# Four heads at a time: chunk bounds from a chunk-per-partition load, bounds in column tiles, and the FFN interleaved in a fixed order

## The chip, the cores and the metric

The kernel runs on one core of a Trainium2 chip. The metric is device time in microseconds (us), where lower is better. The profile is one execution; its span, from the first to the last instruction, is one to two us shorter than the time that is reported. Engines are named as in the profile: PE is the matmul engine (TensorE), PEld its weight loads, which overlap PE (busy 57% and 85% of the span of before), DVE is VectorE, ACT is ScalarE, POOL is GpSimd and SP is SyncE. "Clock" is the TensorE clock that the throttle granted, as a share of full speed; these traces show it at 1.00 or 0.50, and other values are means over a stretch.

A program on one core has no second die to compare with, so a run counts as slow only if it is over 1.5% above the fastest run of the same kernel.

## The reference

The first half is attention with chunk selection, for 4 batches of 8 heads, 768 positions and head size 64. The second half is a gated FFN on the 3072 x 512 result. Cut to what matters:

```python
k_chunks = k.reshape(B, H, 24, 32, 64)                   # 24 chunks of 32 keys
k_min, k_max = k_chunks.min(axis=3), k_chunks.max(axis=3)
ub = sum_d max(q_d * k_min_d, q_d * k_max_d)             # upper bound per query and chunk
ub = where(causal, ub, -1e9)
top_chunks = argsort(ub)[..., -6:]                       # six chunks per query
scores = (q @ k.T) / 8, masked to the selected chunks and to i >= j
x = softmax(scores) @ v                                  # then heads side by side: 3072 x 512
out = (sigmoid(x @ w_gate) * (x @ w_val)) @ w_out        # d_ff = 1536
```

Because max(q k_min, q k_max) is relu(q) k_max + relu(-q) (-k_min), the bound is one matmul with a contraction of 128 rows: relu(q) stacked on relu(-q), against k_max stacked on -k_min. It is done in fp32 in both kernels, since the selection depends on it; everything after it is fp16.

## The kernel before

Work goes head by head, in a software pipeline of three steps. `phase1a` transposes q and k of a head (fp32, on PE), forms the relu stack on ACT and reduces k to chunk bounds on DVE, from the transposed copy in PSUM:

```python
        qkT = pqk.tile([128, S], F32, tag="qkT", name=f"qkT_{hs}")
        for sb in range(NB):                                                   # NB = 6 blocks of 128
            nc.tensor.transpose(qkT[:, 128 * sb:128 * sb + 128], qk_nat[:, sb, :], ident32)
        # ... Qcat = relu(q), relu(-q) on ACT; headK, headQ: fp16 copies on DVE ...
        kTv = qkT[64:128, :].rearrange("p (a c) -> p a c", a=NC)
        nc.vector.tensor_reduce(Kcat[0:64, :], kTv, AX.X, ALU.max)
        nc.vector.tensor_reduce(Kcat[64:128, :], kTv, AX.X, ALU.min, negate=True)
```

`phase1b` makes the bounds and picks six chunks. The queries are the weights here, so six loads of 128 x 128 fp32 weights serve matmuls of only 24 columns each (in the trace each load and each matmul shows as two: 12 of each per head). The picked set goes back through PE into 24 extra rows of the fp16 score operands, so that unselected chunks get a large negative score:

```python
        for qb in range(NB):
            nc.tensor.matmul(ubp[:, qb, :], Qcat[:, 128 * qb:128 * qb + 128], Kcat,
                             start=True, stop=True)
        # ... add the causal penalty, MAX8 per block, compare with the sixth value -> Ap ...
        for qb in range(NB):
            nc.tensor.transpose(ApT[:, 128 * qb:128 * qb + 128], Ap[:, qb, :], ident16)
        nc.vector.tensor_copy(headQ[64:88, :], ApT)
```

`phase2` computes transposed scores per key block, adds the causal mask of the diagonal block with an extra matmul, and multiplies with v:

```python
                nc.tensor.matmul(sc, headK[:, 128 * jb:128 * jb + 128], headQ[:, i0:i1],
                                 start=True, stop=not has_diag)
                if has_diag:
                    off = 128 * jb - i0
                    nc.tensor.matmul(sc[:, off:off + 128], ident16, tneg, start=False, stop=True)
                a_t = attnp.tile([128, n], F16, tag="attnT", name=f"at_{hs}_{jb}_{i0}")
                nc.scalar.activation(a_t, sc, AF.Exp)
        # ... 21 matmuls of 65 columns: attention times value; normalise; transpose pairs of heads ...
```

The FFN of a batch becomes available when its eighth head is done. The main loop issues five FFN units as a block after each head until the queue is empty; 30 units last for six of the eight heads:

```python
    for i in range(NHEADS + 2):
        # ... phase1b(i - 1), phase2(i - 2), loads, phase1a(i) ...
        nunits = min(len(pending_ffn), 5) if i < NHEADS else len(pending_ffn)
        for _ in range(nunits):
            pending_ffn.pop(0)()
```

The softmax here doesn't subtract the row's maximum and nothing guards it: scores larger than these inputs give would overflow.

Of the kernel before, what the change touches and what calls it, by code (L numbers as in the profile page):

```python
# [8 lines left out]
F32 = mybir.dt.float32  # L10
F16 = mybir.dt.float16
BF16 = mybir.dt.bfloat16
# [4 lines left out]
NEG = -30000.0  # L17
# [3 lines left out]
def kernel(  # L21
# [15 lines left out]
    NB = S // 128  # L37
    D_FF = moe_w_gate.shape[1]
    NFB = D_FF // 128
    scale = 1.0 / (D ** 0.5)  # L40
    NHEADS = B * H

    consts = ctx.enter_context(tc.tile_pool(name="consts", bufs=1))
    stage = ctx.enter_context(tc.tile_pool(name="stage", bufs=3))
    persist = ctx.enter_context(tc.tile_pool(name="persist", bufs=1))
    att = ctx.enter_context(tc.tile_pool(name="att", bufs=3))
    smalls = ctx.enter_context(tc.tile_pool(name="smalls", bufs=6))
    attnp = ctx.enter_context(tc.tile_pool(name="attnT", bufs=20))
    xpool = ctx.enter_context(tc.tile_pool(name="xpool", bufs=8))
    xnatp = ctx.enter_context(tc.tile_pool(name="xnat", bufs=2))  # L50
    hglup = ctx.enter_context(tc.tile_pool(name="hglu", bufs=26))
    pqk = ctx.enter_context(tc.tile_pool(name="pqk", bufs=1, space=bass.MemoryType.PSUM))
    pa = ctx.enter_context(tc.tile_pool(name="pa", bufs=5, space=bass.MemoryType.PSUM))
    pb = ctx.enter_context(tc.tile_pool(name="pb", bufs=1, space=bass.MemoryType.PSUM))
# [5 lines left out]

    tneg = consts.tile([128, 128], F16, tag="tneg")
    nc.gpsimd.memset(tneg, 0.0)
    nc.gpsimd.affine_select(
        out=tneg, in_=tneg, compare_op=ALU.is_ge, fill=NEG,
        base=0, pattern=[[1, 128]], channel_multiplier=-1,
    )
    Epat = consts.tile([24, NC, CH], F16, tag="Epat")
    nc.gpsimd.memset(Epat, 0.0)
    nc.gpsimd.affine_select(
        out=Epat, in_=Epat, compare_op=ALU.not_equal, fill=NEG,  # L70
        base=0, pattern=[[-1, NC], [0, CH]], channel_multiplier=1,
    )
    Edram = nc.dram_tensor("E_scratch", (24, S), F16, kind="Internal").ap()
    nc.sync.dma_start(Edram, Epat.rearrange("a b c -> a (b c)"))
    pen = consts.tile([24, NC, CH], F32, tag="pen")
# [3 lines left out]
        base=0, pattern=[[1, NC], [0, CH]], channel_multiplier=-1,  # L79
    )  # L80
    pen2 = consts.tile([128, NB, 24], F32, tag="pen2")
    penv = pen.rearrange("a b c -> a (b c)")
    for qb in range(NB):
        p2ps = pa.tile([128, 24], F32, tag="m", name=f"pen2t_{qb}")
        nc.tensor.transpose(p2ps, penv[:, 128 * qb:128 * qb + 128], ident32[0:24, 0:24])  # L85
        nc.vector.tensor_copy(pen2[:, qb, :], p2ps)  # L86

    wg16 = persist.tile([128, 4, D_FF], F16, tag="wg16")
    wv16 = persist.tile([128, 4, D_FF], F16, tag="wv16")
    wo16 = persist.tile([128, NFB, 512], F16, tag="wo16")  # L90
    _wunits = []
    for sl, dst, nchunk in ((moe_w_gate, wg16, 4), (moe_w_val, wv16, 4), (moe_w_out, wo16, NFB)):
        src = sl.rearrange("(c p) f -> p c f", p=128)
        for c in range(nchunk):
            def _load(src=src, dst=dst, c=c):
                st = stage.tile([128, src.shape[2]], F32, tag="wstage")
                nc.sync.dma_start(st, src[:, c, :])
                nc.scalar.copy(dst[:, c, :], st)  # L98
            _wunits.append(_load)

    def score_chunks(jb):
        lo = 128 * jb
        if jb == 0:
            return [(0, 384), (384, 768)]
        if jb == 1:
            return [(128, 384), (384, 768)]
        return [(lo, 768)]

    st1 = {}
    xT = {}  # L110
    xnat = {}
    hgl_tiles = {}

    def phase1a_dma(hs):
        b, hh = divmod(hs, H)
        d = {}
        qk_nat = stage.tile([128, NB, 128], F32, tag="qk_nat", name=f"qknat_{hs}")
        nc.sync.dma_start(qk_nat[:, :, 0:64], q[b, hh].rearrange("(sb p) d -> p sb d", p=128))
        nc.sync.dma_start(qk_nat[:, :, 64:128], k[b, hh].rearrange("(sb p) d -> p sb d", p=128))
        v_nat = stage.tile([128, NB, 64], F32, tag="v_nat", name=f"vnat_{hs}")  # L120
        nc.sync.dma_start(v_nat, v[b, hh].rearrange("(sb p) d -> p sb d", p=128))
        d["qk_nat"] = qk_nat
        d["v_nat"] = v_nat
        return d

    def phase1a(hs, d):
        b, hh = divmod(hs, H)
        qk_nat = d["qk_nat"]
        v_nat = d["v_nat"]
        v16 = att.tile([128, NB, 65], F16, tag="v16", name=f"v16_{hs}")  # L130
        nc.gpsimd.tensor_copy(v16[:, :, 0:64], v_nat)
        nc.gpsimd.memset(v16[:, :, 64:65], 1.0)
        d["v16"] = v16

        qkT = pqk.tile([128, S], F32, tag="qkT", name=f"qkT_{hs}")
        for sb in range(NB):
            nc.tensor.transpose(qkT[:, 128 * sb:128 * sb + 128], qk_nat[:, sb, :], ident32)  # L137
        Qcat = stage.tile([128, S], F32, tag="Qcat", name=f"Qcat_{hs}")
        nc.scalar.activation(Qcat[0:64, :], qkT[0:64, :], AF.Relu)  # L139
        nc.scalar.activation(Qcat[64:128, :], qkT[0:64, :], AF.Relu, scale=-1.0)  # L140
        headK = stage.tile([88, S], F16, tag="headK", name=f"headK_{hs}")
        nc.sync.dma_start(headK[64:88, :], Edram)
        nc.vector.tensor_scalar(headK[0:64, :], qkT[64:128, :], scale, None, ALU.mult)
        headQ = stage.tile([88, S], F16, tag="headQ", name=f"headQ_{hs}")
        nc.vector.tensor_copy(headQ[0:64, :], qkT[0:64, :])
        Kcat = stage.tile([128, 24], F32, tag="Kcat", name=f"Kcat_{hs}")
        kTv = qkT[64:128, :].rearrange("p (a c) -> p a c", a=NC)
        nc.vector.tensor_reduce(Kcat[0:64, :], kTv, AX.X, ALU.max)
        nc.vector.tensor_reduce(Kcat[64:128, :], kTv, AX.X, ALU.min, negate=True)  # L149
        d["Qcat"] = Qcat  # L150
        d["Kcat"] = Kcat
        d["headK"] = headK
        d["headQ"] = headQ

    def phase1b(hs, d):
        Qcat, Kcat, headQ = d["Qcat"], d["Kcat"], d["headQ"]
        ubp = pb.tile([128, NB, 24], F32, tag="ub", name=f"ub_{hs}")
        for qb in range(NB):
            nc.tensor.matmul(ubp[:, qb, :], Qcat[:, 128 * qb:128 * qb + 128], Kcat,  # L159
                             start=True, stop=True)  # L160
        ubm = smalls.tile([128, NB, 24], F32, tag="ubm", name=f"ubm_{hs}")
        nc.vector.tensor_tensor(ubm, ubp, pen2, ALU.add)
        mx8 = smalls.tile([128, NB, 8], F32, tag="mx8", name=f"mx8_{hs}")
        for qb in range(NB):
            nc.vector.max(mx8[:, qb, :], ubm[:, qb, :])
# [88 lines left out]
    for i in range(NHEADS + 2):  # L254
        if 1 <= i <= NHEADS:
            phase1b(i - 1, st1[i - 1])
# [47 lines left out]
```

## Time and profile before

| | before |
|---|---|
| time, median of the 3 runs given | 513.81 us (508.92 to 516.24) |
| span of the profile, mean clock | 510.6 us, 0.852 |
| busy | PE 85%, DVE 52%, ACT 44%, POOL 4% |
| first stage, attention of batch 0 alone | 111 us |
| three mixed stages, attention of a batch with the FFN of the one before | 120 + 119.5 + 109.5 us |
| final stage, FFN of batch 3 alone | 50.6 us |

The stages of before are cut where the first FFN matmul of each batch starts (111, 231, 350.5 and 460 us), just behind the last output transpose of the batch before. The prediction below used slightly other cuts (114, 233, 353, 472).

From the page of before: busy time by engine (us, share of the span, instructions), then two rows of the 40 slices of the span (12.8 us each; digits are tenths), the chain of waits that ended last by engine, and one group of matmuls (busy us, mean ns of one, idle before it).

```profile
PE 436.1 (85%) x3046; PEld 289.7 (57%) x3046; DVE 267.8 (52%) x678; ACT 222.3 (44%) x461; POOL 22.9 (4%) x78
...
PE   2665988889799798889889799788979889889997
...
PEclk9976667659989899568979989766979989969999
...
PE 57%; DVE 21%; ACT 15%; issue 6%; POOL 1%; ACTq 0%; POOLq 0%
...
L159 PE MATMUL ub_3179<-Kcat_3100,Qcat_3092 128*128 128x24 f32 x12 | 2.8, 389 | 1.4 <-DVE Kcat_3100 L149 1.4
```

From the table of stretches of before (stretch in us and its length, then busy us and instructions of each engine, mean clock, share of the DMA engines, GB/s):

```profile
core 0: us, PE busy (x) PEld busy (x) DVE busy (x) ACT busy (x) POOL busy (x), PEclk, DMA share, GB/s
0.00:111.00 111.00, 78.22 (x549) 61.14 (x550) 64.62 (x167) 58.14 (x105) 10.95 (x36) 0.74 0.60 161
111.00:231.00 120.00, 107.03 (x763) 70.53 (x762) 66.60 (x169) 50.67 (x110) 4.54 (x16) 0.86 0.22 56
231.00:350.50 119.50, 106.50 (x762) 70.25 (x761) 66.54 (x169) 50.66 (x110) 4.54 (x16) 0.86 0.22 56
350.50:460.00 109.50, 97.50 (x715) 62.11 (x714) 56.34 (x149) 47.47 (x106) 2.84 (x10) 0.90 0.11 31
460.00:510.60 50.60, 46.86 (x265) 25.69 (x263) 13.72 (x28) 15.37 (x30) 0.00 (x0) 0.99 0.08 32
207.00:216.00 9.00, 8.25 (x50) 6.45 (x51) 5.13 (x19) 4.19 (x9) 0.00 (x0) 0.50 0.28 65
234.00:256.00 22.00, 20.11 (x164) 12.94 (x162) 13.99 (x29) 12.94 (x29) 0.57 (x2) 1.00 0.21 48
```

PE is the bound, but its busy share hides a second question. The last two lines have PE equally busy, 92% and 91%, and yet the clock was 0.50 in the one and 1.00 in the other. From 207 to 216 us the FFN queue has run dry and there is only attention; from 234 to 256 us there is FFN. Part of the 92% is the half clock itself, at which the same matmuls last longer (a set of 12 bounds matmuls took 2.75 us at 206.5 us, on a clock of 0.50, and 1.52 us at 247.9 us, on 1.00): in the 7.7 us just before the clock fell (198.5 to 206.2 us) PE was busy 74% at 1.00. So in this trace the busy share alone does not say how close PE is to its full rate.

To separate work from clock, I scale each matmul's time until the next by the clock over it (four bounds matmuls follow the last four after 0.27 us at 1.00 and 0.53 us at 0.50, both in after). By this estimate, in the three mixed stages PE was busy 311 us for 269.5 us of full-clock work, and idle 38 us. So of their 349 us, 41.6 us are lost to the clock and 38 us to waits.

### The profile page before, as it was taken

The numbers are of one execution on the slowest core, as the hardware profiler recorded it, in microseconds if no ns is written. First come the engines' busy times: TensorE is split into PE (matmuls) and PEld (weight loads), VectorE is DVE, ScalarE is ACT, GpSimd is POOL, SyncE is SP. The second block draws the span as 40 slices with busy tenths as digits, with TensorE's granted clock in tenths as the row PEclk, the third lists the DMA queues.
The fourth block names the chain that finished last, engine by engine and source line by source line (L and its number), as shares of the span: only waits on it lengthen the run. The fifth ranks groups of instructions, "written<-read, shape, count | busy, mean of one in ns | idle before, by whom it ended". The sixth has DMA issues, their size and how long they took to land.

```text
span 510.6 us, 8014 instructions
## 1 busy us (share of the span) xinstructions
PE 436.1 (85%) x3046; PEld 289.7 (57%) x3046; DVE 267.8 (52%) x678; ACT 222.3 (44%) x461; POOL 22.9 (4%) x78
## 2 busy tenths in 40 slices
PE   2665988889799798889889799788979889889997
PEld 1544766666556555666565555566655555555553
DVE  3445568755725644664742844674661765434140
ACT  2266477525415454434515433461533524443231
POOL 5000000000000000000000000000000000000000
PEclk9976667659989899568979989766979989969999
DMA  9776455312203223220203102230221100100101
GB/s 180 245 226 214 118 144 156 88 27 51 50 23 90 50 50 94 52 66 23 59 20 111 43 16 84 70 83 17 51 50 62 35 4 4 63 1 1 44 19 63
DMA packets 82826, 36.34 MB, mean 71 GB/s; under 512 B 76364, under 2 KB 77156, under 8 KB 82788
## 3 DMA queue, kind: packets, MB, share of 16 engines
q1 hardware_dynamic: 82788, 35.83, 26.2%
q8 instruction: 24, 0.39, 0.3%
q14 instruction: 14, 0.11, 0.1%
HBM read 29.49 MB, written 6.33 MB: 70 GB/s over the span
## 4 chain that ended last, share of the span: by engine, by line
PE 57%; DVE 21%; ACT 15%; issue 6%; POOL 1%; ACTq 0%; POOLq 0%
ACT wg_136 L98 1%; PE ub_5312 L159 1%; PE ub_4212 L159 1%; PE ub_3179 L159 1%; PE ub_2783 L159 1%; PE ub_1750 L159 1%; PE ub_619 L159 1%; PE ub_2464 L159 1%; PE ub_4608 L159 1%; PE ub_1354 L159 1%; PE ub_3893 L159 1%; PE ub_352 L159 1%; PE ub_227 L159 1%; PE ub_175 L159 1%; PE ub_495 L159 1%
## 5 line engine op out<-in xcount | busy, mean ns | idle before, releaser
L227 PEld LDWEIGHTS <-wv_137 128*128 128x128 f16 x384 | 39.4, 102 | 28.6 <-issue 6.1
L221 PEld LDWEIGHTS <-wg_136 128*128 128x128 f16 x384 | 39.1, 105 | 25.3 <-issue 6.0
L186 PEld LDWEIGHTS <-ident_96 128*128 128x128 f16 x192 | 21.7, 113 | 10.9 <-issue 6.3
L98 ACT CAST wo_138<-st 128x512 f16<-128x512 f32 x12 | 7.3, 647 | 2.2 <-DMA st<-in_moe_w_out_dram 2.1
L98 ACT CAST wg_136<-st 128x1536 f16<-128x1536 f32 x4 | 5.8, 1470 | 5.4 <-DMA st<-in_moe_w_gate_dram 5.4
L159 PE MATMUL ub_352<-Kcat_340,Qcat_332 128*128 128x24 f32 x12 | 2.7, 387 | 4.9 <-ACT wg_136 L98 4.9
L159 PE MATMUL ub_227<-Kcat_224,Qcat_216 128*128 128x24 f32 x12 | 2.7, 387 | 4.9 <-DVE Kcat_224 L149 4.9
L159 PE MATMUL ub_175<-Kcat_172,Qcat_164 128*128 128x24 f32 x12 | 2.7, 387 | 4.3 <-DVE Kcat_172 L149 4.3
L98 ACT CAST wv_137<-st 128x1536 f16<-128x1536 f32 x4 | 5.9, 1487 | 0.3 <-DMA st<-in_moe_w_val_dram 0.3
L137 PE MATMUL qkT_157<-ident_91,qknat_139 128*128 128x128 f32 x6 | 1.5, 422 | 4.7 <-DMA qknat_139<-in_k_dram 4.7
L159 PEld LDWEIGHTS ub_227<-Kcat_224,Qcat_216 128*128 128x128 f32 x12 | 2.6, 329 | 5.1 <-issue 5.1
L159 PE MATMUL ub_495<-Kcat_483,Qcat_475 128*128 128x24 f32 x12 | 2.7, 387 | 3.3 <-DVE Kcat_483 L149 3.3
L159 PEld LDWEIGHTS ub_352<-Kcat_340,Qcat_332 128*128 128x128 f32 x12 | 2.6, 330 | 5.0 <-ACT wg_136 L98 5.0
L159 PEld LDWEIGHTS ub_495<-Kcat_483,Qcat_475 128*128 128x128 f32 x12 | 2.6, 329 | 4.4 <-ACT wv_137 L98 4.4
L159 PEld LDWEIGHTS ub_175<-Kcat_172,Qcat_164 128*128 128x128 f32 x12 | 2.6, 329 | 4.4 <-issue 4.4
L230 DVE SCALAR_TENSOR_TENSOR hg_384_0_5711<-gate_384_0_5704,vv_384_0_5706 128x384 f16<-128x384 f16 x1 | 0.6, 554 | 8.5 <-PE vv_384_0_5706 L227 8.5
L171 DVE COPY headQ_3098<-ApT_3197 24x768 f16<-24x768 f16 x1 | 0.5, 549 | 7.6 <-PE ApT_3197 L170 7.6
L171 DVE COPY headQ_4527<-ApT_4626 24x768 f16<-24x768 f16 x1 | 0.5, 548 | 7.6 <-PE ApT_4626 L170 7.6
L171 DVE COPY headQ_1669<-ApT_1768 24x768 f16<-24x768 f16 x1 | 0.5, 548 | 7.6 <-PE ApT_1768 L170 7.6
L139 ACT ACTIVATE Qcat_216<-qkT_209 64x768 f32<-64x768 f32 x1 | 0.8, 804 | 8.4 <-PE qkT_209 L137 8.4
L86 DVE COPY pen_117<-pen2t_118 128x24 f32<-128x24 f32 x1 | 0.2, 184 | 7.4 <-PE pen2t_118 L85 7.4
L159 PE MATMUL ub_3179<-Kcat_3100,Qcat_3092 128*128 128x24 f32 x12 | 2.8, 389 | 1.4 <-DVE Kcat_3100 L149 1.4
(3469 smaller groups left out, 1546.1 us busy)
## 6 DMA issues: line engine op xcount, KB each, us to landing
st<-in_moe_w_gate_dram SPq DMA_DIRECT2D x4, 768.0 KB
st<-in_moe_w_val_dram SPq DMA_DIRECT2D x4, 768.0 KB
st<-in_moe_w_out_dram SPq DMA_DIRECT2D x12, 256.0 KB
out_dram<-osb_0_0_1715 SPq DMA_DIRECT2D x1, 256.0 KB
out_dram<-osb_0_1_1731 SPq DMA_DIRECT2D x1, 256.0 KB
out_dram<-osb_0_2_1747 SPq DMA_DIRECT2D x1, 256.0 KB
out_dram<-osb_384_0_2295 SPq DMA_DIRECT2D x1, 256.0 KB
out_dram<-osb_384_1_2311 SPq DMA_DIRECT2D x1, 256.0 KB
```

The lines of the kernel that those rows point to most:

```text
L86: nc.vector.tensor_copy(pen2[:, qb, :], p2ps)
L98: nc.scalar.copy(dst[:, c, :], st)
L137: nc.tensor.transpose(qkT[:, 128 * sb:128 * sb + 128], qk_nat[:, sb, :], ident32)
L139: nc.scalar.activation(Qcat[0:64, :], qkT[0:64, :], AF.Relu)
L159: nc.tensor.matmul(ubp[:, qb, :], Qcat[:, 128 * qb:128 * qb + 128], Kcat, start=True, stop=True)
L171: nc.vector.tensor_copy(headQ[64:88, :], ApT)
L186: nc.tensor.matmul(sc[:, off:off + 128], ident16, tneg, start=False, stop=True)
L221: nc.tensor.matmul(g_ps, wg16[:, c, 128 * fb:128 * fb + 128], xT[(b, c)][:, t0:t0 + TCH], start=(c == 0), stop=(c == 3))
L227: nc.tensor.matmul(v_ps, wv16[:, c, 128 * fb:128 * fb + 128], xT[(b, c)][:, t0:t0 + TCH], start=(c == 0), stop=(c == 3))
L230: nc.vector.scalar_tensor_tensor(hgl, gate, 1.0, v_ps, ALU.add, ALU.mult)
```

## The change

The intent is to treat four heads as a group. Keys are loaded a second time with one chunk per partition (4 heads x 24 chunks = 96 partitions), so that chunk bounds of four heads come from two reduces, without transposing k in fp32. The bounds matmul is turned round: the 32-wide block of chunk bounds of a head is the weight, the queries stream by 320 columns, and the four heads go to the four 32-column tiles of the array (128*32 in the trace). The diagonal mask moves from PE to GpSimd. The first 128 queries skip selection, as they can see at most four chunks. FFN units are merged one by one among the attention tasks of a group, in a fixed order weighted by cost. The core of it, with cuts:

```diff
+        d["kc"] = kcp.tile([96, CH, D], F32, tag="kc", name=f"kc_{g}")
+        nc.sync.dma_start(d["kc"], k[b, h0:h0 + 4].rearrange("h (c s) d -> (h c) s d", s=CH))
 # ... q, k, v of the group follow in 256-byte pieces; k is cast to fp16 on GpSimd ...
+        kv = d["kc"].rearrange("p s d -> p d s")
+        nc.vector.tensor_reduce(kmm[:, 0:64], kv, AX.X, ALU.max)
+        nc.vector.tensor_reduce(kmm[:, 64:128], kv, AX.X, ALU.min, negate=True)
-        nc.vector.tensor_reduce(Kcat[0:64, :], kTv, AX.X, ALU.max)
-        nc.vector.tensor_reduce(Kcat[64:128, :], kTv, AX.X, ALU.min, negate=True)
 # ...
-        for qb in range(NB):
-            nc.tensor.matmul(ubp[:, qb, :], Qcat[:, 128 * qb:128 * qb + 128], Kcat,
-                             start=True, stop=True)
+        hw = 64 * NQ                                              # 320
+        for x in range(2):
+            for h in range(4):
+                nc.tensor.matmul(ps[32 * h:32 * h + 32, x, 0:hw], kcat[g % 2][:, h, :],
+                                 d[("qcat", h)][:, hw * x:hw * x + hw], start=True, stop=True)
 # ...
-                if has_diag:
-                    nc.tensor.matmul(sc[:, off:off + 128], ident16, tneg, start=False, stop=True)
+        if x == 1:
+            nc.gpsimd.affine_select(out=dv, in_=dv, compare_op=ALU.is_ge, fill=0.0,
+                                    base=0, pattern=[[0, NB], [1, 128]], channel_multiplier=-1)
 # ...
+    def merge(a, f):                                              # a: attention tasks, f: FFN units
+        for c, t in a:
+            t()
+            done_a += c
+            while fi < len(f) and done_f + f[fi][0] / 2 <= tf * done_a / ta:
+                f[fi][1]()
+                done_f += f[fi][0]
+                fi += 1
-        nunits = min(len(pending_ffn), 5) if i < NHEADS else len(pending_ffn)
-        for _ in range(nunits):
-            pending_ffn.pop(0)()
```

Group g+1 is prepared (casts, bounds, selection) between the score tasks of group g. Weights are loaded and cast by GpSimd's DMA queue instead of by SyncE and ACT. PSUM is split into three pools: three buffers for the FFN and three for attention, of up to 128 x 512 fp32 each, and one of 128 x 1024 for the fp32 steps.

## The prediction

> **What bounds the kernel now.** TensorE. The page's busy line gives PE 436.1 of 510.6 us (85%), DVE 52%, ACT 44%; in the chain of waits PE has 57%. The table of stretches shows: 0 to 114 us (first batch's attention, no FFN to fill in; PE busy 81, clock 0.73), three repeats of about 119 us (PE busy 106-107, clock 0.86-0.91), 39 us of pure FFN (clock 0.99). The clock is 1.00 at 234-256 us (FFN mixed in) but 0.50 at 207-216 and 221-233, where the FFN queue has run dry (PE still 90% busy). [...]
>
> Scaling each PE line's time by the granted clock, 436 us are 371 at full clock: FFN 189, bounds matmul 45, scores 38, attention-times-value 33, fp32 transposes 28, diagonal mask 17, selection transposes 14, output transposes 6.
>
> **Removed, added, moved (full-clock PE us).** Diagonal mask 17 -> 0 (to GpSimd, about 1 us per head, hidden). Bounds 45 -> about 20: today 112 ns per half matmul for 24 columns, so the weight load is what is paid; after, 64 matmuls of 320 columns. [...] that is 4.3 us per group if serial (34 in all), 1-1.5 if the four column tiles overlap; I take the middle. fp32 transposes 28 -> 14 (128 at 109 ns; k's bounds come from a reduce over the per-chunk load). New: 192 fp16 feature transposes at 62 ns, 12. Selection transposes 14 -> 3. Sum about 315.
>
> ACT stays near 225 us; DVE falls from 268 to about 215; Pool rises to about 80.
>
> **On the critical path.** In the three mixed stages PE work is 47.3 (FFN) + 2 x 14.5 = 76 us; at 90% filling about 86 instead of 119, with the clock near 1.0 because FFN is spread evenly. That is most of the gain. The final FFN stays about 48.
>
> The first stage gains little. Pool waits for q, then k, then v before sending more weight loads, PE transposes the second group's q before it scores the first, and Pool casts the second group's q and k before it masks the first head. So group 0 cannot finish before the second load lands. From the trace, 256-byte packets move about 227 GB/s: 12.7 us per group load, about 25 us for weights: about 50 us in all. Then 16 us for the rest of group 0 and 26 for group 1 (ACT 21 us per group, half clock): about 93, against 114.
>
> Total: 93 + 3 x 86 + 48 - 4 (last group prepares nothing) = 395 us.
>
> **Predicted: 395 us, 368 to 425 (8 in 10). Faster by over 2%: 0.97; within 2%: 0.02; slower: 0.01.**
>
> **What would show it.** PE busy 325-350 us; mean clock 0.85 -> about 0.93, half clock only before 100 us; mixed stages of 80-90 us; bounds matmuls 1-4.5 us per group (do column tiles overlap?); first exp after 30 us, PE idle on q's second load near 40 us; final FFN 48 us.
>
> **What would make it wrong.** Single-buffered PSUM, passed between ACT, DVE and PE, could stall PE in the mixed stages (95-100 us each, total near 430), or three FFN banks be too few. Fully overlapping column tiles and a first stage of 75 us would give 365. GpSimd masking late would lengthen the first stage.

FFN 189, scores 38, values 33, bounds 20, fp32 transposes 14, feature transposes 12, output transposes 6 and selection transposes 3 are the 315 us. The 4.3 us can be had from the trace of before, as an estimate: five fp32 transposes of 128 columns stand 0.11 us apart (at 250.75 us, clock 1.00), and at that rate 16 passes of 320 columns are 4.4 us, a fourth of it 1.1. That the weight load was paid for fits the same trace: 12 bounds passes of 24 columns (at 247.9 us) stand 0.11 us apart, as those of 128 columns do, and their weight loads keep PEld busy for 1.41 of the set's 1.52 us.

The 227 GB/s are the 18 ns that a 256-byte packet took in before (median), on 16 DMA engines; the 6 KB packets of its weights took 234 ns by the median and 271 by the mean, or 420 and 363 GB/s. From these, 2.4 MB in small packets and 0.8 MB in large ones for a group load come to 12.2 to 12.5 us, and 9.4 MB of weights to 22 to 26 us; both are estimates.

## The result, and the profile after

| | before | after |
|---|---|---|
| median of the runs made together | 512.87 us (508.92 to 516.24, 4 runs) | 393.81 us (392.42 to 395.26, 4 runs) |
| ratio of the fast runs | | 0.769 (0.764 to 0.773) |
| span, mean clock | 510.6 us, 0.852 | 393.6 us, 0.926 |
| PE busy; DVE; ACT; POOL | 436; 268; 222; 23 us | 320; 230; 205; 74 us |
| first / mixed / final stage | 111 / 349 / 50.6 us | 109.6 / 233.6 / 50.4 us |

A ratio is the mean time of one kernel's fast runs over that of the other's of the same rounds, so it is not quite the ratio of the medians quoted. The interval is of 95%. The output was correct.

From the page after, the same lines (slices of 9.8 us each), and two groups:

```profile
PE 320.2 (81%) x2696; PEld 197.2 (50%) x2696; DVE 230.0 (58%) x486; ACT 204.6 (52%) x393; POOL 73.5 (19%) x77
...
PE   1071549287598999799979998799999999999996
...
PEclk9996557856969999999999999999999999999999
...
PE 58%; DVE 17%; ACT 8%; issue 6%; SPq 5%; DMA 4%; POOL 1%; ACTq 0%; DVEq 0%; POOLq 0%
...
L153 PE MATMUL qT_0_369<-ident_103,q_176 128*128 128x128 f32 x5 | 1.3, 426 | 5.8 <-DMA q_176<-in_q_dram 5.8
...
L261 PE MATMUL pv_0_401<-v_141,att_0_335 128*128 128x65 f16 x21 | 1.3, 244 | 4.5 <-POOL att_0_335 L249 4.5
```

From the table of stretches after: the first stage in parts, the three mixed stages, the final one, and two short stretches in which a set of bounds matmuls runs. Here the stages are cut at the last output transpose of each batch (109.6, 190.9, 273.6 and 343.2 us, to within 0.2 us). The first FFN matmul would not do as a cut: in after some of them run as early as 68.5 us, long before the program issues them. So something between the program and PE, the build or the engine, moves them; the trace does not say which.

```profile
core 0: us, PE busy (x) PEld busy (x) DVE busy (x) ACT busy (x) POOL busy (x), PEclk, DMA share, GB/s
0.00:44.00 44.00, 11.33 (x71) 7.60 (x72) 29.83 (x59) 9.58 (x13) 15.26 (x25) 0.87 1.16 205
44.00:66.00 22.00, 15.07 (x126) 9.45 (x125) 10.41 (x14) 12.41 (x24) 7.33 (x7) 0.57 1.13 215
66.00:80.00 14.00, 6.12 (x87) 4.68 (x85) 13.61 (x36) 5.80 (x10) 3.74 (x3) 0.88 0.42 95
80.00:109.60 29.60, 22.65 (x215) 15.22 (x214) 21.29 (x47) 18.33 (x35) 9.15 (x8) 0.73 1.06 184
109.60:190.90 81.30, 75.13 (x658) 46.03 (x656) 53.87 (x114) 49.02 (x96) 17.64 (x15) 0.95 0.47 104
190.90:273.60 82.70, 74.61 (x679) 45.90 (x675) 55.60 (x116) 50.47 (x98) 13.23 (x12) 1.00 0.19 49
273.60:343.20 69.60, 68.49 (x617) 42.68 (x615) 31.51 (x78) 43.30 (x88) 7.13 (x8) 1.00 0.06 24
343.20:393.60 50.40, 46.78 (x265) 25.62 (x262) 13.85 (x25) 15.68 (x31) 0.00 (x0) 1.00 0.10 37
59.00:62.00 3.00, 2.85 (x18) 0.64 (x18) 2.97 (x2) 1.67 (x4) 0.86 (x1) 0.50 1.14 207
25.00:29.00 4.00, 3.29 (x23) 1.14 (x23) 0.53 (x2) 2.77 (x4) 0.00 (x0) 1.00 1.23 233
```

The first and the final stage hardly moved. All of the gain is in the three mixed stages: 349 us became 233.6, each now at a clock of 0.95 to 1.00. The first stage's PE row, with digits of 0, 1 and 2, is full of holes. The two groups above name two of them: PE waits for the DMA of the second group's q (5.8 us, until 35 us) and for GpSimd's mask before the first values (4.5 us). The table of stretches shows a third: from 66 to 80 us DVE is busy 13.61 of 14.00 us and PE only 6.12.

By line, PE's work at full clock went from 371 to 301 us: bounds 45 to 10.7, attention-times-value 33 to 20.5, diagonal mask 17 to 0, all transposes 48 to 37, FFN 189 to 192 and scores 38 to 40. The prediction had about 315. (Both totals are somewhat too high, for the reason told below under the clock record.)

The DVE reduces that replace those of before are the new long instructions. The next line lists the first reduce (the maximum) of one group (minimum, median and maximum ns, then the start in us):

```profile
L140 DVE TENSOR_REDUCE kmm_721<-kc_683 x1: 3697/3697/3697, 59.3 to 59.3; 96x64 f32<-96x2048 f32 x1
```

All sixteen of them took between 3.55 and 3.74 us. That is 1.73 to 1.82 ns for each of the 2048 elements of a partition, which are read at a stride of 64 elements (256 bytes). There are two for each group.

**A limit of the clock record.** From 25 to 29 us the table says 1.00, but the bounds matmuls there took 741 ns each, as much as from 59 to 62 us, where it says 0.50; in later groups at full clock they took 438 ns. The packed trace explains it: its first clock event, in after at 28.8 us and in before at 28.7, is a change to full clock (the first to half follows at 32 us). Before the first event there is no record, and the views count that as 1.00, while the matmuls ran at half rate. Mean clocks of whole runs share this flaw; I rest nothing on the clock of the first stage. From the first event on, durations and records agree.

### The profile page after: what moved, and what is told of

It reads as the page before. It is cut to its first block, busy times and chain, and to the rows that moved or that the text cites. A ratio compares the mean times of both kernels' runs of the same rounds, so it can differ in the third digit from the quotient of the medians.

```text
span 393.6 us, 6906 instructions
## 1 busy us (share of the span) xinstructions
PE 320.2 (81%) x2696; PEld 197.2 (50%) x2696; DVE 230.0 (58%) x486; ACT 204.6 (52%) x393; POOL 73.5 (19%) x77
## 3 DMA queue, kind: packets, MB, share of 16 engines
q1 hardware_dynamic: 79616, 31.47, 37.3%
## 4 chain that ended last, share of the span: by engine, by line
PE 58%; DVE 17%; ACT 8%; issue 6%; SPq 5%; DMA 4%; POOL 1%; ACTq 0%; DVEq 0%; POOLq 0%
SPq L125 5%; DMA k_177<-in_k_dram 3%; DMA kc_151<-in_k_dram 2%; DVE kmm_1096 L140 1%; DVE kmm_209 L140 1%; DVE kmm_721 L141 1%; DVE kmm_1096 L141 1%; DVE kmm_209 L141 1%; PE o_0_0_2626 L296 1%; PE o_0_0_3781 L296 1%; PE o_384_0_3203 L296 1%; PE o_384_0_2048 L296 1%; PE o_0_0_1471 L296 1%; PE o_384_2_4783 L296 1%; PE o_384_1_4298 L296 1%
## 5 line engine op out<-in xcount | busy, mean ns | idle before, releaser
L287 PEld LDWEIGHTS <-wv_146 128*128 128x128 f16 x384 | 37.9, 99 | 28.3 <-issue 4.2
L281 PEld LDWEIGHTS <-wg_145 128*128 128x128 f16 x384 | 35.7, 99 | 23.2 <-issue 6.7
L153 PE MATMUL qT_0_212<-ident_103,q_148 128*128 128x128 f32 x5 | 1.3, 426 | 8.4 <-DMA q_148<-in_q_dram 8.4
L243 PEld LDWEIGHTS <-hk_123 96*128 96x128 f16 x48 | 4.8, 122 | 3.8 <-issue 2.9
L153 PE MATMUL qT_1_227<-ident_103,q_148 128*128 128x128 f32 x5 | 1.3, 427 | 5.9 <-DVE qcat_1_221 L160 5.9
L153 PE MATMUL qT_0_369<-ident_103,q_176 128*128 128x128 f32 x5 | 1.3, 426 | 5.8 <-DMA q_176<-in_q_dram 5.8
L140 DVE TENSOR_REDUCE kmm_1096<-kc_1044 96x64 f32<-96x2048 f32 x1 | 3.7, 3667 | 3.7 <-PE kct_756 L146 3.7
L272 PE MATMUL xps_1_671<-ident_108,xnat_400 128*128 128x128 f16 x6 | 0.8, 307 | 6.1 <-DVE xnat_400 L265 6.1
L140 DVE TENSOR_REDUCE kmm_209<-kc_151 96x64 f32<-96x2048 f32 x1 | 3.6, 3591 | 3.8 <-DMA kc_151<-in_k_dram 3.8
L272 PEld LDWEIGHTS <-xnat_400 128*128 128x128 f16 x24 | 2.1, 120 | 7.2 <-DVE xnat_400 L265 6.9
L243 PEld LDWEIGHTS <-hk_135 96*128 96x128 f16 x48 | 4.3, 109 | 2.4 <-issue 1.1
L243 PEld LDWEIGHTS <-hk_125 96*128 96x128 f16 x48 | 4.5, 110 | 1.9 <-issue 0.5
L193 PEld LDWEIGHTS <-ap_140 128*128 128x128 f16 x20 | 1.5, 106 | 7.7 <-DVE ap_140 L187 6.1
L193 PE MATMUL apT_316<-ident_108,ap_140 128*128 128x128 f16 x5 | 0.7, 309 | 5.7 <-DVE ap_140 L187 5.7
L243 PEld LDWEIGHTS <-hk_131 96*128 96x128 f16 x48 | 4.1, 107 | 2.3 <-issue 1.1
L243 PEld LDWEIGHTS <-hk_133 96*128 96x128 f16 x48 | 4.3, 108 | 1.8 <-issue 0.2
L153 PEld LDWEIGHTS qT_0_212<-ident_103,q_148 128*128 128x128 f32 x5 | 0.9, 220 | 8.3 <-issue 8.3
L140 DVE TENSOR_REDUCE kmm_359<-kc_179 96x64 f32<-96x2048 f32 x1 | 3.6, 3597 | 2.4 <-DMA kc_179<-in_k_dram 2.4
L261 PE MATMUL pv_0_401<-v_141,att_0_335 128*128 128x65 f16 x21 | 1.3, 244 | 4.5 <-POOL att_0_335 L249 4.5
L243 PEld LDWEIGHTS <-hk_127 96*128 96x128 f16 x48 | 4.2, 106 | 1.6 <-issue 0.2
```

The source lines that it names most:

```text
L140: nc.vector.tensor_reduce(kmm[:, 0:64], kv, AX.X, ALU.max)
L153: nc.tensor.transpose(ps[:, 128 * i:128 * i + 128], d["q"][:, i + 1, 2 * pr:2 * pr + 2, :].rearrange("p h d -> p (h d)"), ident32)
L193: nc.tensor.transpose(ps[:, 128 * i:128 * i + 128], apt[g % 2][:, i, :, :].rearrange("p h c -> p (h c)"), ident16)
L243: nc.tensor.matmul(ps[:, o:o + w], hk[:, 128 * jb:128 * jb + 128], hq[:, i0:i0 + w], start=True, stop=True)
L261: nc.tensor.matmul(ps[:, ib, :], at[:, c:c + 128], v16s[g % 2][:, jb, h, :], start=(jb == 0), stop=(jb == ib))
L272: nc.tensor.transpose(ps[:, 128 * ib:128 * ib + 128], xnat[b][:, ib, 128 * c:128 * c + 128], ident16)
```

## The experiments

The control for the experiments on after is the ratio of after itself, 0.769. `a_bounds_serial` below does the same work and gave 0.7688 in other rounds, so the control repeats. "First stage" and "mixed" are times between the same points of the program as in the table above, to within 0.2 us.

### Spreading the FFN over all eight heads, in before

```diff
-        nunits = min(len(pending_ffn), 5) if i < NHEADS else len(pending_ffn)
+        nunits = min(len(pending_ffn), (3, 4, 4, 4)[i % 4]) if i < NHEADS else len(pending_ffn)
```

> The kernel before, with one change: 30 FFN units of a batch are issued 3 or 4 per head over all 8 heads instead of 5 per head over the first 6. Total work is the same. Theory 'even filling keeps the clock up': in before, each of the three mixed stages (about 119 us) has about 25 us at half clock after the FFN queue has run dry; now the half clock should vanish from the mixed stages (clock 0.86-0.91 to above 0.95), PE busy falls from 436 to about 405 us and the time by 25 to 40 us (to about 475-490). Rival 'only the removed work counts, the spread does not': within 2% of before. In-between: the clock rises but the time falls less, since the waits of the serial transposes and bounds remain.

Measured: correct, 497.42 us (496.27 to 498.49), ratio 0.971 (0.967 to 0.975). The mean clock stayed at 0.855, and the row of the clock still has its holes. The prediction gave "FFN is spread evenly" as the reason for a high clock. Spreading it evenly over heads, still as a block after each head, gives 3% and does not bring the clock back. So that reason, as it was put, is not enough. The trace shows what the edit left: in the mixed stages PE still ran for up to 14.8 us without any FFN matmul, and 140 us in all in stretches of over 5 us, against 150 us before.

### FFN units one by one within each head, in before

```diff
+    def some_ffn(n):
+        for _ in range(min(n, len(pending_ffn))):
+            pending_ffn.pop(0)()
 # in phase2, between the scores and the values of a head:
+        some_ffn(1)
         pvp = pa.tile([128, NB, 65], ...)
 # in the loop, after phase1b and after phase2:
+            some_ffn(1)
-        nunits = min(len(pending_ffn), 5) if i < NHEADS else len(pending_ffn)
+        nunits = min(len(pending_ffn), (0, 1, 1, 1)[i % 4]) if i < NHEADS else len(pending_ffn)
```

> The kernel before with its FFN units set singly at four places of each head's work (after the bounds, between scores and values, after the values, after the next head's transposes), and spread over all heads. Fine-interleave theory: half clock falls from 151 us to under 90, time 450 to 480 us. Rival 'what attention consists of sets the clock': half clock stays above 125 us, time 485 to 500 us, like the variant that is only spread over the batch (497).

Measured: correct, 447.42 us (446.92 to 452.24), ratio 0.876 (0.871 to 0.881). The clock row of its page, with slices of 11.1 us, and the mixed stages in its table of stretches:

```profile
PEclk9996665656999999999999999999999999999999
```

```profile
110.40:207.40 97.00, 91.76 (x763) 60.58 (x761) 68.06 (x178) 51.37 (x111) 4.54 (x16) 0.99 0.29 71
207.40:303.20 95.80, 90.17 (x762) 59.92 (x761) 65.71 (x169) 50.45 (x110) 4.54 (x16) 1.00 0.28 70
303.20:394.50 91.30, 85.39 (x714) 55.24 (x713) 53.52 (x140) 46.24 (x105) 2.85 (x10) 1.00 0.12 36
```

The instruction counts are those of before: no work was removed. Still the clock is at full speed in all three mixed stages, which fall from 349 to 284 us. The first and last stages, 110.4 and 50.6 us, are those of before. With the scaling by the clock, the mixed stages split like this (us):

| mixed stages | length | PE work at full clock | lost to the clock | PE idle |
|---|---|---|---|---|
| before | 349.0 | 269.5 | 41.6 | 38 |
| before, FFN in single units | 284.1 | 266.2 | 1.2 | 17 |
| after | 233.6 | 214.3 | 3.9 | 15 |

With no work removed, spreading and single units together are worth 65 of the 119 us: 40 from the clock, 21 from filled waits and 3 of shorter PE work (spreading in blocks alone gave 15, `b_even`). The other 50 us between this kernel and after are, to within 2 us, less work on PE at full clock: in the mixed stages bounds 22 us, transposes 14 and the mask 14, and little else. The split of the first row into the second is shown by an experiment on before; that after owes the same part to its interleave is inferred from the equal clock. The next two runs were meant to test it in after, and did so only in part.

The traces of before, `b_even` and this run give a simple sign of when the clock falls: how long PE runs without an FFN matmul. I list the stretches between two FFN matmuls in the mixed stages, for these and the next two runs (us):

| mixed stages of | longest stretch without FFN | sum of those over 5 us | lost to the clock |
|---|---|---|---|
| before | 32.5 | 150 | 42 |
| `b_even` | 14.8 | 140 | 32 |
| `b_fine` | 5.2 | 5 | 1 |
| after | 2.7 | 0 | 4 |
| `a_clump` | 8.5 | 17 | 9 |
| `a_coarse` | 2.8 | 0 | 2 |

In before and `b_even` the record goes to half clock in each of the 17 stretches of over 9 us, 4 to 10 us after it began, and in one of the seven of 5 to 6 us. Not every half-clock record has such a stretch: after has one from 165 to 169 us without. PE was also less busy in these stretches (70 to 83%), so whether it is the kind of work or its thinness that counts is not separated.

### FFN that runs out within a group, in after

Of a batch's FFN two thirds go to the first of the two groups that it accompanies, and the last third is issued at double rate in the second, so that the second half of that group should have none. The trace shows less than that: FFN matmuls moved into the gap, and the longest stretch without them was 8.5 us, at the end of each of the first two mixed stages.

```diff
-    def merge(a, f):
+    def merge(a, f, rate=1.0):
-            while fi < len(f) and done_f + f[fi][0] / 2 <= tf * done_a / ta:
+            while fi < len(f) and done_f + f[fi][0] / 2 <= rate * tf * done_a / ta:
-            n = len(ffn) // 2
+            n = 2 * len(ffn) // 3
-        merge(a, parts[g % 2])
+        merge(a, parts[g % 2], 1.0 + g % 2)
```

> The changed kernel with the reverse: two thirds of each batch's FFN in the first of its two groups, the last third packed into the first half of the second group, so that about half a group of attention is left without FFN, as in before. Even-filling theory: half clock comes back in the last part of each of the three mixed stages (some 10 us of each), about 4 to 8 us more per stage, 405 to 418 us in all. Rival: within 1.5% of 393.8.

Measured: correct, 408.74 us (408.09 to 409.66), ratio 0.799 (0.795 to 0.802), mean clock 0.912; mixed stages 86.2, 89.0 and 71.3 us. With such a stretch, the time grows by 3.8% and half-clock time comes back (71.7 us on record, against 58.0): the clock falls 7 us into both stretches, at 195.5 and 284.3 us. In the mixed stages the clock costs 5 us more than in after and idle PE 6 us more. This is the loss of before again, in small.

### FFN after every eleventh attention task, in after

```diff
-        for c, t in a:
+        for k, (c, t) in enumerate(a):
-            while fi < len(f) and done_f + f[fi][0] / 2 <= tf * done_a / ta:
+            while k % 11 == 10 and fi < len(f) and done_f + f[fi][0] / 2 <= tf * done_a / ta:
```

> The changed kernel with FFN units emitted after every eleventh attention task instead of after each: the same units per group, in clumps of about a head. Spreading before's FFN over all heads of a batch (still in clumps per head) took 3% off and left the clock where it was, so the spread over the batch is not what keeps the clock up. Theory 'the fine interleave does it: without FFN for some microseconds the clock is halved, and attention's own waits are bare': half clock comes back in the mixed stages (more than 30 us beyond the 58 us of after), 408 to 430 us. Rival 'the clock is up since the work of attention itself is denser (no narrow fp32 matmuls, fewer and longer pieces)': clock stays, half clock under 70 us, the time under 402 us.

Measured: correct, 397.75 us (397.51 to 398.17), ratio 0.777 (0.774 to 0.780), clock 0.935. As a test of larger blocks the run failed. The edit changes the order in which the program issues FFN, but on PE the mixed stages stay finely mixed: the longest stretch without FFN is 2.8 us (2.7 in after), and attention and FFN alternate 112 times (115 in after). This part of its timeline (start us, us, engine, line, instruction, count) runs from the end of twelve FFN matmuls, `o`, at 223.4 us to the next ones:

```profile
223.20 0.38 PE L243 MATMUL sc<-hq,hk 96*128 96x512 f16 x1
223.42 0.80 PE L261 MATMUL pv<-v,att 128*128 128x65 f16 x21
224.06 0.38 PE L243 MATMUL sc<-hq,hk 96*128 96x512 f16 x1
224.54 0.50 PE L203 MATMUL f<-ident,q 128*128 128x128 f16 x6
224.87 0.59 PE L296 MATMUL o<-wo,hg 128*128 128x512 f16 x2
```

Nor did it cost the mixed stages anything: they took 231 us against 233.6. The 1% lies in the final stage, 56.5 us against 50.4, into which 28 more FFN matmuls were left over. So whether after would keep its clock with longer stretches of attention alone was not tested; where stretches of 8.5 us came about, in the run before this one, the clock fell. The rival named in the expectation, that attention in after is itself denser, stays untested too.

One place looks denser. In before, the values matmuls of a head come in bursts, each waiting for the next exp; in after they come as one run. From the timelines (in brackets the wait before the instruction), first before, then after:

```profile
255.43 0.20 PE L198 MATMUL pv_3033<-v_17_2692,at_2_256_3016 128*128 128x65 f16 x1 [0.16 <-ACT at_2_256_3016 L188]
```

```profile
199.00 0.80 PE L261 MATMUL pv_0_2335<-v_141,att_0_2213 128*128 128x65 f16 x21
```

This fits with this work having shrunk from 33 to 20.5 us at full clock, though its matmuls are 672 in both. But it is no property of after's attention alone: with an FFN unit set between scores and values, before does it too (`b_fine`: 23.7 us, the 21 matmuls of a head in one run).

### The bounds on the full array, in after

Each head's bounds are padded with zeros to 128 columns and the four heads accumulate into one result: the same numbers from 16 matmul passes (each of the 8 fp32 matmuls shows as two), each over all 128 columns. They stood one behind the other, 4.47 us for a group.

```diff
-                nc.tensor.matmul(ps[32 * h:32 * h + 32, x, 0:hw], kcat[g % 2][:, h, :],
-                                 d[("qcat", h)][:, hw * x:hw * x + hw], start=True, stop=True)
+                nc.tensor.matmul(ps[:, x, 0:hw], kcat[g % 2][:, 128 * h:128 * h + 128],
+                                 d[("qcat", h)][:, hw * x:hw * x + hw], start=h == 0, stop=h == 3)
```

> The changed kernel with the bounds matmuls on the full array: each head's weights stand in their own 32 of 128 otherwise zero columns and the four heads accumulate into one output, so that the same result comes from 8 matmuls a group that cannot run beside each other (one more small ScalarE copy a group). Exchanging the loops had not taken the overlap away. Theory 'the overlap of the column tiles is worth about 3 us a group': a group's bounds take about 4.3 us at full clock instead of 1.1 to 1.3, PE busy rises by some 25 us, and the time by 15 to 28 us (408 to 422). Rival 'the mixed stages wait on the passing of the single transposing buffer between engines, not on PE': PE busy rises as much, the time by under 8 us.

Measured: correct, 410.02 us (406.81 to 410.99), ratio 0.800 (0.795 to 0.804). In after, a set of 16 passes stood on the timeline as below: four matmuls start within 20 ns, and the next four 0.29 us later.

```profile
124.61 0.46 PE L169 MATMUL ubT_1291<-qcat_0_1126,kcat_142 128*32 128x320 f32 x1
124.62 0.46 PE L169 MATMUL ubT_1291<-qcat_1_1129,kcat_142 128*32 128x320 f32 x1
124.62 0.46 PE L169 MATMUL ubT_1291<-qcat_2_1228,kcat_142 128*32 128x320 f32 x1
124.63 0.46 PE L169 MATMUL ubT_1291<-qcat_3_1231,kcat_142 128*32 128x320 f32 x1
124.90 0.43 PE L169 MATMUL ubT_1291<-qcat_0_1126,kcat_142 128*32 128x320 f32 x1
```

So the column tiles overlap fully: four passes follow the last four after 0.27 us, as single passes do on the full array, and a group takes 1.3 us at full clock, where the full array took 4.47 us. On the full array the bounds took 37.6 us at full clock over the run, against 10.7, a factor of 3.5. The overlap saves 27 us of PE work and 16 us of time. The first stage, where PE waits much of the time anyway, grew by only 3.6 us; the mixed ones grew by 3.4, 6.0 and 2.7 us.

### The bounds matmuls in another order, in after

```diff
-        for x in range(2):
-            for h in range(4):
+        for h in range(4):
+            for x in range(2):
```

> The changed kernel with the two loops of the bounds matmuls exchanged (head outside, half of the columns inside), so that neighbouring matmuls use the same column tile; every other instruction of every engine stays in the same order. In the trace of after, four heads' half matmuls start within 30 ns of each other and the set of 16 takes about 1.1 us at full clock. Theory 'the column tiles overlap and that is where the bounds' gain comes from': with the same tile in a row, a group's bounds take 3 to 4.3 us at full clock, and the time rises by about 2 to 3 us per group in the seven groups that prepare another, some 12 to 22 us in all (406 to 416). Rival 'the gain is only that 8 wide matmuls replace 24 narrow ones': the same time within 1%.

Measured: correct, 393.77 us (392.60 to 394.82), ratio 0.769 (0.766 to 0.772). The set of 16 passes still took 1.30 us:

```profile
123.82 1.30 PE L169 MATMUL ubT<-qcat,kcat 128*32 128x320 f32 x16
```

The edit was meant to put two matmuls of the same tile side by side and so to end the overlap. It did not end it: the trace still shows four sets of four, within 40 ns in each set and 0.23 to 0.25 us between the sets. The names in this trace do not tell the heads apart, so in which order PE ran them, and what undid the written order, can't be told. As a test of the overlap the run failed, and the full-array run above took its place.

### The diagonal mask back on PE, in after

```diff
-                             start=True, stop=True)
+                             start=True, stop=i0 != 128 * jb)
+            if i0 == 128 * jb:
+                nc.tensor.matmul(ps[:, o:o + w], ident16, tneg, start=False, stop=True)
-        if x == 1:
-            nc.gpsimd.affine_select(out=dv, in_=dv, ...)
```

> The changed kernel with the diagonal mask back on TensorE (192 matmuls of the identity with a triangle, as before) and no mask on GpSimd. The prediction called the mask on GpSimd hidden and worth 17 us of PE. Each such matmul is about 64 ns: 12 us of PE, 1.5 us a group. Theory: the mixed stages grow by 1 to 2 us a group (6 to 11 us in all), but in the first stage the values of head 0 no longer wait for the mask (53 us in after, its exponentials done at 46), since GpSimd first casts group 1's q and k: first stage 3 to 8 us shorter; in all 391 to 402. If the mask on GpSimd costs nothing anywhere, the time is 402 to 408; if GpSimd's queue is what makes the first stage 110 us long, it is under 388.

Measured: correct, 401.39 us (399.92 to 401.94), ratio 0.783 (0.779 to 0.787). The mask costs PE 11.5 us at full clock (60 ns for each of the 192 matmuls), and moving it to GpSimd is worth about 7.6 us. The first stage stayed at 109.3 us. So GpSimd's late mask, which the profile after shows as a wait of 4.5 us before the first values, is not what makes that stage long.

### The chunk reduces over contiguous data, in after (a wrong result)

```diff
-        kv = d["kc"].rearrange("p s d -> p d s")
+        kv = d["kc"].rearrange("p s d -> p (s d)").rearrange("p (d s) -> p d s", d=D)
```

The same 2048 elements are reduced in the same groups of 32, but groups are contiguous, so the bounds are those of the wrong elements and the output is wrong (relative error 0.576). The work of all the other instructions is the same.

> Wrong result on purpose: the two reduces over a chunk read their 32 elements side by side instead of 256 bytes apart; the same count, the same order of all instructions. In after one takes 3.6 us, or 1.75 ns an element, where the reduce of before took 1.25 ns an element. Theory 'the stride makes the reduce slow, and the slow reduce sits in the chain of the first stage and stalls PE in the mixed ones': each falls to about 2.2 us, the first stage (110 us) by 6 to 10 us, groups of the mixed stages by 1 to 2 us each, the whole by 10 to 18 us (376 to 384). Rival 1 'the reduce costs that anyway': still 3.6 us and the same time. Rival 2 'DVE is off the critical path': 2.2 us each, but the time within 1%.

Measured: 379.24 us (378.28 to 380.44), ratio 0.741 (0.737 to 0.744). The first of its two groups by line (busy us, mean ns, idle before):

```profile
L140 DVE TENSOR_REDUCE kmm<-kc 96x64 f32<-96x2048 f32 x8 | 18.2, 2278 | 12.0 <-DMA kc<-in_k_dram 8.3 <-PE kct L146 3.7
```

The reduce falls to 2.28 us, 1.11 ns per element, and the time falls by 14.6 us: 3.4 us in the first stage, and 6.0 and 5.5 us in the first two mixed stages. The third mixed stage, in which no such reduce runs any more (the last one starts at 244 us), is unchanged at 69.6 us. The stride was the cost, and it lay on the critical path, although DVE is busy only 58% of the time: in the mixed stages PE's idle time fell from 15 to 6 us. Why a strided read is slower is not shown.

### Weights after the second group's casts, in after

```diff
         last = nc.gpsimd.tensor_copy(v16s[g % 2][:, :, :, 0:64], d["v"])
+        if g == 1:
+            with tc.issue_after(last.ins):
+                ... load_w(0..2), load_wo(0..2)
```

> The changed kernel with the nine weight loads queued behind the casts of the second group. First stage of after: 110 us; group 0's first exponential at 44 us, behind the load of group 1's q (35 us) and k (51 us), which share the DMA engines with the weights. Theory 'the first stage waits for group 1's loads, and the weights slow these': q of group 1 lands some 8 to 15 us earlier, first exponential before 36 us, the first stage 8 to 20 us shorter, 374 to 386 us in all. Rival 1 'DVE sets the first stage (eight reduces of 3.6 us in its chain)': the loads land earlier but the stage shrinks by under 5 us. Rival 2: the weights, now later, are late for the first FFN units, and the gain is given back (over 390 us).

Measured: correct, 398.60 us (396.23 to 401.01), ratio 0.778 (0.773 to 0.784). The first scores came at 39.0 us instead of 42.9, but the first stage took 112.1 us instead of 109.6. The chain of waits of this run shows it waiting later, at 80 to 88 us, for the load of a later group's q, with a mask of GpSimd queued behind the cast of it. The first mixed stage grew as well, from 81.3 to 84.3 us. So group 0 did begin 4 us earlier, and more than that was given back. That the weights share the DMA engines with the loads is shown in after: the packets of both queues are counted on the same 16 engines (37.3% and 7.2% of their span), and a 256-byte packet took 31 ns (median) at 20 to 30 us, with weights on the way, and 18 ns at 50 to 66 us, without. Weights are not the only cause: at 80 to 110 us, again without them, it was 24 ns.

### GpSimd's masks ahead of its casts, in after

```diff
-        nc.gpsimd.tensor_copy(d["k16"], d["k"])
+        with tc.issue_after(M[(g - 1, 0)].ins) if g else ExitStack():   # M: the masks
+            nc.gpsimd.tensor_copy(d["k16"], d["k"])
 # ... the casts of q and v likewise
```

> The changed kernel with one rule of order: the casts of a group queue on GpSimd behind the mask of the former group's first head, so that no mask waits for a load of a later group. Delaying the weight loads had not helped: group 0 began earlier, but its values waited until 89 us for a mask behind a cast of group 3's q. Theory 'GpSimd's in-order queue sets the first stage': values of head 0 start before 48 us (53.5 in after), the first stage falls from 110 by 6 to 15 us, the mixed stages stay: 380 to 388. Rival 'DVE's chain (reduces, picks, sign copies) sets the first stage': under 3 us gained, 390 to 396.

Measured: correct, 393.24 us (392.35 to 394.48), ratio 0.768 (0.764 to 0.771). The first values came at 49.7 us instead of 53.5, and the first stage still ended at 109.3 us. The 4.5 us wait for the mask is therefore not the limit of that stage.

### All instructions in program order, in after

```diff
-    with _tile.TileContext(nc) as tc:
+    with _tile.TileContext(nc, linearize=True) as tc:
 # and load(1) after the preparation of group 0 instead of before it
```

> The changed kernel issued strictly in program order on every engine[...]; the second group's load stands after the first group's preparation. Theory 'pulling later groups' work ahead costs the first stage, and the written merge is a good order by itself': first exponential before 38 us (44), first stage under 100 us, in all 372 to 388. Rival 'the scheduler's order fills gaps that the written order leaves': mixed stages over 86 us each, in all over 396.

Measured: correct, 1648.74 us (1638.30 to 1649.86), ratio 3.22. PE was busy 38% of a span of 1636.6 us, and the busy shares of PE, DVE, ACT and POOL add up to only 71%: the engines hardly ran beside each other. The option took away the overlap and not only the reordering, so the run says nothing about the order. It failed as an experiment.

### The chunk bounds by halving, in after

Maximum and minimum are taken by halving with elementwise operations over contiguous halves (1024, 512, 256, 128 and 64 elements), which needs no strided read. To make room, the causal penalty is kept in bfloat16.

```diff
-        nc.vector.tensor_reduce(kmm[:, 0:64], kv, AX.X, ALU.max)
-        nc.vector.tensor_reduce(kmm[:, 64:128], kv, AX.X, ALU.min, negate=True)
+        for o, op in ((0, ALU.max), (64, ALU.min)):
+            r = sel.tile([96, CH // 2, D], F32, tag="tree", name=f"tree_{g}_{o}")
+            nc.vector.tensor_tensor(r, d["kc"][:, 0:16, :], d["kc"][:, 16:32, :], op)
+            for n in (8, 4, 2):
+                nc.vector.tensor_tensor(r[:, 0:n, :], r[:, 0:n, :], r[:, n:2 * n, :], op)
+            nc.vector.tensor_tensor(kmm[:, o:o + 64], r[:, 0, :], r[:, 1, :], op)
+        nc.vector.tensor_scalar(kmm[:, 64:128], kmm[:, 64:128], -1.0, None, ALU.mult)
```

> The changed kernel with a correct way round the slow strided reduce: maximum and minimum over a chunk's 32 rows by halving, five two-input steps each on rows that lie side by side (1984 elements for each of the two, and one sign change of 64); the causal penalty constant is kept in bfloat16 to make room. The wrong-on-purpose reduce without stride took DVE's 7.2 us a group to 4.5 us and the time from 393.8 to 379.2, while queueing GpSimd's casts behind the masks moved nothing. [...] Theory 'DVE's reduce time is what counts': 380 to 386 us, full-preparation groups of the mixed stages at about 39 us instead of 41.4, first stage about 107. Rival 'eleven small instructions are broken up by DVE's other work[...]': 388 us or more.

Measured: correct, 379.77 us (376.73 to 380.75), ratio 0.738 (0.733 to 0.742). Its groups by line:

```profile
L143 DVE TENSOR_TENSOR tree<-tree 96x512 f32<-96x512 f32 (+2 forms) x48 | 28.6, 596 | 0.8
L141 DVE TENSOR_TENSOR tree<-kc 96x1024 f32<-96x1024 f32 x16 | 19.5, 1219 | 6.2 <-DMA kc<-in_k_dram 5.8
```

The first stage took 104.8 us and the mixed ones 77.5, 76.8 and 69.6 us, much as with the contiguous reduce, and here with the right result. The halving itself takes DVE 55.2 us in all (the two groups above and 5.6 and 1.5 us for the last steps), where the 16 reduces took 58.1. So DVE hardly works less; it works in eleven pieces per group instead of two, and other DVE work can go between them. That this is the reason is argued from these numbers; no run separates it. This version beats both kernels, after by 3.6% and before by 26%.

## Why the prediction was right, point by point

**Right: the bound and the total.** The prediction said 395 us, and the median was 393.81. PE was the bound, and the time fell in the mixed stages: 115 of the 117 us of span. PE busy came to 320 us, just under the band of 325 to 350, and the mean clock to 0.926 against "about 0.93", though whole-run means carry the flaw told above. The final FFN took 50 us, as before.

**The total hides two errors that cancel.** The sum was 93 + 3 x 86 + 48 - 4 = 395. Measured were 109.6 + (81.3 + 82.7 + 69.6) + 50.4 = 394. The first stage was put 17 us too low and the mixed stages 20 us too high (254 after the 4 us taken off, against 233.6).

**The first stage (93 predicted, 110 measured).** The waits that were named did occur: PE idle on the second group's q at 35 us, the first exp only at 44 us. And the second group's k landed at 51 us, near the 50 us put for the loads. But from there the stage took another 58.6 us where 42 were put: 26 for group 1 and 16 for the rest of group 0, estimates from PE and ACT alone. DVE's chain was left out: 13.61 of 14 us busy at 66 to 80 us, with reduces of 3.6 us ahead of the copies that PE waits for. The contiguous reduce and the halving took 3 to 5 us off that stage; moving the mask to PE, or GpSimd's masks forward, took nothing off. What paces the remaining 105 us, DVE's shorter work or the loads, stays open; the one attempt on the loads gave back what it gained.

**The mixed stages (86, 86, 82 predicted; 81, 83, 70 measured).** The filling was right: 90% was assumed, and PE was busy 92%, 90% and 98%. Three terms of the work were mis-sized. The bounds were put at "the middle", about 20 us, and the column tiles overlapped fully: 10.7 us. Attention-times-value was kept at 33 us, and took 20.5 without the bursts (most of that came in before too, once FFN stood between scores and values). And the end was credited only 4 us for having nothing to prepare. The two groups of the second mixed stage took 41.4 and 41.3 us with PE busy 37.3; the next, which has no reduce left, took 37.8 with 36.8 busy; the last, which prepares nothing, 31.8 with 31.7 busy. So preparation costs about 10 us a group, 6 of PE and 4 of waiting.

**The clock: right in size, its reason too coarse.** The prediction had the clock near 1.0 "because FFN is spread evenly". Spread evenly over heads in blocks, before gained 3% and kept its clock at 0.855, with up to 14.8 us without FFN left; spread in single units it ran at 0.99 to 1.00, with none over 5.2 us. So it is the fineness of the mix and not evenness over a batch that brought the clock back in before (65 us, with the filled waits). After, with none over 2.7 us, fits; that it would lose its clock without the mix is shown only in small, by `a_clump`. The two rates show in the record (1.00 and 0.50) and in the matmuls (sets of four bounds matmuls start 0.27 and 0.53 us apart). What sets the clock could not be read from busy time: PE was busy 74% in the 7.7 us before it fell (before, 198.5 to 206.2 us), and 72% over 8 us without a fall (after, 198 to 206 us).

**Smaller checks.** "Half clock only before 100 us" was nearly right: some remains until about 114 us and again from 165 to 169 us. The bounds took 1.3 us per group at full clock, within 1 to 4.5. DVE fell to 230 us, not 215, and ACT to 205, not 225: the strided reduces probably cost more than was allowed for (58 us, and 41 at the 1.25 ns an element of before's reduces), and ACT no longer casts the weights (19 us in before). A shortage of PSUM, named as what could make it wrong, did not occur: PE was idle only 15 us in all three mixed stages.

## What to carry to other kernels

Where an engine is the bound but its trace shows a lowered clock, try, before removing any work, to mix what ran at full clock into what did not, in single units: in the kernel before, an edit of a few lines that did so with the FFN took the clock of the mixed stages from between 0.86 and 0.90 to between 0.99 and 1.00 and gave 12%. Check in the trace that an edit of the order reached the engine: of the experiments on after, one left the mix on PE as it was, another changed it only in part, and a third left the overlap that it was to end. Read stages and not averages: DVE was busy 58% and still cost 14 us, because two long strided reduces stood ahead of short copies that the bound engine waited for. When a predicted total comes out right, check its terms, as here two errors of 17 and 20 us cancelled.
